# Batches 2 to 7 of a fused attention and bilinear feed-forward kernel: heads grouped by row halves, fewer turning products, and token sums on partitions from batch 2

## The chip, the cores and the metric

The kernel runs on one core of one Trainium2 chip. The metric is the device time of one execution in microseconds (us), as the median of the runs. The engines are TensorE (PE, with its weight loads shown apart as PEld), VectorE (DVE), ScalarE (ACT), GpSimd (POOL) and SyncE (SP).

## The reference

For 8 batches of 8 heads with 576 tokens, head size 64 and 32 memory slots, `phi` gives softmax weights over the slots, and with these every slot gets a mean of the keys and a mean of the values. The queries attend over the 32 slot means. The result, 4608 tokens of 512, goes through a bilinear feed-forward layer with 1536 inner columns.

```python
a = softmax(phi)                               # over the 32 slots, per token
k_m = einsum('bhsm,bhsd->bhmd', a, k)          # means of keys
v_m = einsum('bhsm,bhsd->bhmd', a, v)          # means of values
attn = softmax(q @ k_m.T / sqrt(64))           # (b, h, 576, 32)
x = (attn @ v_m) -> (4608, 512)
out = ((x @ w_a) * (x @ w_b)) @ w_out          # 512 -> 1536 -> 512
```

## The kernel before

The inputs come in by DMA from the POOL queue in a fixed order (`p`, `k`, `v`, `q` of a batch, `w` for columns of w_a and w_b, `o` for w_out). On the chip everything is in 16 bits, and each head's rows lie on 64 partitions: a tile holds two heads per column group, head `2*hp+r` on the partitions from `64*r`, with `r` 0 or 1 and `hp` 0 to 3.

The four stages of a batch are these. **Means:** `kv_sums` (line 277) multiplies the exponentials of `phi` with keys, values and a column of constants, on PE tiles of 64 rows by 32 columns: `tile_position=(64*r, 32*j)` for head slot `j` of group `g`. Two groups of four heads fill two PSUM banks `pkv`. `take_kv` (306) divides by the sums and writes copies into `rep`; `kv_transpose` (321) turns `rep` on PE into `pT`, and DVE copies that to `kvT`, from which each head finds its means on the partitions on which its queries or its weight rows lie. Batches 0 and 1 use other functions for this (`sums`, `transpose`, lines 329 and 353).

**Attention:** `scores` (363) multiplies turned queries with `kvT` on PE tiles of 32 by 32; `exp_scores` writes the exponentials `E`, with slots on partitions and tokens along the row. In batches 0 to 3 the sums over the 32 slots come from PE: `denominators` (391) multiplies `E` with a block matrix of ones into `pD`, ACT takes the logarithm into `L`, and `normalise` (401) has ACT make the reciprocal `R` and DVE (batches 0, 1) or POOL (2, 3) the product `A`. In batches 4 to 7 DVE turns `E` in 32x32 blocks (`e_turn`, 414), so that tokens lie on partitions; `token_sums` (422) reduces and takes reciprocals on DVE, `token_normalise` (429) multiplies, the first part on POOL and the second on DVE, and `a_turn` (435) turns back.

**Up:** `fold` (439) multiplies the value means with rows of w_a and w_b, and `take_fold` (456) moves the product to `vab`; `up_half` (618) multiplies `vab` with `A` into `pa` and `pb`, ACT copies `pa`, and DVE multiplies it with `pb` into the tile `ht`.

**Down:** two chunks of 128 tokens at a time go through w_out with seven products in place of eight (`two_downs`, 542); the sums of blocks that this needs are `w_sums` (`sum_weights`, 512) and `h_sums` (`sum_tokens`, 525).

The order of the work on all engines is written out in the list `PLAN`. In it `2kv` means the means of batch 2, `2km` and `2kvt` the copies and the turning, `2sc` scores, `2e0` exponentials, `2den0` and `2nr0` sums by PE and normalising, `2ed`, `2sm0`, `2tn0`, `2ad` the way by tokens, `2v0` and `2x0a` folding, `a2.3.0` and `b2.3.0` an up product, `dN` N matmuls of the down stage, `h` or `g` a `h_sums` on POOL or DVE, `T` or `V` a `w_sums` on POOL or DVE, `F` and `f` filling matmuls at the start that keep the TensorE clock up. Each engine executes its part of the list in order.

The function that orders the heads decides which rows of the array a head uses:

```python
def head(g, j):
    jj = j ^ g
    return jj % 2, 2 * g + jj // 2     # r, hp
```

So the four heads of a group lie on both row halves by turns.

Of the kernel before, what the change touches and what calls it, by code (L numbers as in the profile page):

```python
# [9 lines left out]
F16 = mybir.dt.float16  # L10
# [3 lines left out]
P = 128  # L14
# [11 lines left out]
f3 F1 O 0exp0 f1 f1 F2 p1 f2 f6 F7 w0:256 f2 f1 k1 f1 F3 0exp1 F5 f2 0qt0 q1.0 0ks0 0ks1 F5 0kt0 0qt1 M F2 0s0  # L26
w256:512 0qt2 0kt1 0e0 0den00 0qt3 0s1 0e1 F4 0den01 1exp0 0vs0 q1.1 0vt0 v1 0vs1 1exp1 F6 0nr00 0den10 0vt1
0den11 0hv0a 0hx0a 0nr10 0hv0b 0hx0b 0nr11 a0.1.0 b0.1.0 a0.0.0 F4 0nr01 1ks0 1ks1 b0.0.0 0hv1a 0hx1a 1kt0 1kt1
1qt0 1qt1 a0.0.1 a0.2.1 F1 b0.0.1 1s0 a0.1.1 0hv1b 1qt2 1qt3 0hx1b 1s1 1e0 1e1 b0.2.1 1den0 a0.2.0 b0.1.1 b0.2.0
1den1 1vs1 1vs0 1vt1 1nr0 1vt0 1nr1 a0.3.1 a0.3.0 1hv1b 1hx1b 1hv0b 1hv0a 1hx0a w512:1024 1hx0b b0.3.1 b0.3.0  # L30
1hv1a 0v1a 1hx1a 0x1a a1.0.0 a1.1.1 a1.1.0 a1.0.1 b1.0.0 b1.1.1 b1.1.0 a1.3.0 b1.0.1 a1.3.1 b1.3.0 b1.3.1 a0.5.0
0v1b 1v1a w1024:1536 0x1b 1x1a a1.2.0 1v1b 0v2a 1x1b o1 0x2a a0.7.1 b0.5.0 b1.2.0 b0.7.1 a0.7.0 b0.7.0 o5 a1.5.0
a1.2.1 b1.2.1 b1.5.0 a0.4.0 a0.6.0 b0.4.0 a0.4.1 a1.4.0 b0.6.0 b1.4.0 a0.9.1 0v2b 1v2b 1v2a 0x2b 1x2b a1.5.1
b0.4.1 1x2a b0.9.1 a0.8.0 a1.4.1 b1.5.1 o2 a0.5.1 a0.6.1 b0.8.0 a0.9.0 b0.6.1 b0.9.0 b1.4.1 a1.7.1 b0.5.1 b1.7.1
a0.8.1 b0.8.1 o0 a1.7.0 a0.10.0 b1.7.0 b0.10.0 a0.11.0 a1.9.0 o3 o4 b0.11.0 g0.0 b1.9.0 a1.6.1 k2 a1.6.0 p2 h0.3
a0.11.1 b1.6.1 b0.11.1 a1.8.1 a0.10.1 b1.6.0 v2 b1.8.1 g0.1 T01 a1.8.0 T00 V20 q2 T21 d1 2exp0 a1.9.1 d3 b0.10.1
p3 a1.10.0 d2 V10 g0.2 V11 d1 b1.9.1 2exp1 d1 a1.11.1 k3 d1 q3 T31 T30 d1 b1.10.0 b1.8.0 d1 b1.11.1 d4 h1.0 d2
2kv d4 2km d3 a1.11.0 d10 a1.10.1 2qt0 3exp0 d1 2kvt d2 h1.1 d1 2qt1 d12 2qt2 d3 2qt3 b1.10.1 g1.2 b1.11.0 v3 d1
2sc 2e0 d1 g1.3 d3 g2.0 d3 2e1 d1 2den0 h2.1 d8 p4 d8 2nr0 2den1 g2.2 2v0 2x0a 2x0b d2 2nr1 d10 2v1 d5 2x1a 3qt0
d3 g2.3 d3 2x1b d1 a2.3.0 a2.2.0 b2.3.0 b2.2.0 q4 k4 v4 a2.5.0 3exp1 b2.5.0 d2 3qt1 d4 a2.0.0 b2.0.0 d3 h3.0  # L40
a2.1.0 a2.4.0 2v2 3kv 3qt3 2x2a 3qt2 b2.1.0 2x2b d2 a2.11.1 a2.6.0 d4 3km a2.8.0 d1 q5 b2.4.0 d3 b2.6.0 d2 4exp0
d5 b2.11.1 d5 h3.1 d2 b2.8.0 a2.11.0 3kvt d2 a2.8.1 a2.7.1 b2.8.1 d2 a2.9.0 b2.7.1 3sc 3e1 3e0 g3.3 d1 b2.11.0
4qt0 a2.7.0 d2 a2.5.1 b2.5.1 b2.7.0 h3.2 3den0 d1 3nr0 4qt3 d1 b2.9.0 d2 a2.0.1 4qt2 a2.10.0 b2.0.1 p5 a2.4.1
b2.10.0 d1 k5 a2.10.1 d3 b2.10.1 d3 h4.0 4exp1 d1 a2.2.1 b2.4.1 3den1 d4 3v1 3x1a 4kv 3v0b 3x1b d3 3x0b d1 3nr1
d6 4km0 h4.1 a2.6.1 b2.2.1 a2.9.1 4qt1 a2.1.1 3v0a 3v2 d1 3x0a d2 3x2a d2 b2.6.1 3x2b d4 a3.9.0 d4 a3.5.0 d2
4km1 h4.2 b2.9.1 d1 a2.3.1 4kvt d1 b2.1.1 d1 b2.3.1 d2 5qt0 4sc a3.11.0 d1 h4.3 b3.5.0 5qt2 d5 4e1 d1 4e0 d1 v5
d6 b3.9.0 a3.0.0 g5.0 d1 h5.1 d3 4ed b3.11.0 d1 a3.3.0 d2 a3.10.1 b3.0.0 h5.2 5exp0 4sm0 q6 a3.1.0 d1 b3.3.0 d4
a3.3.1 d2 p6 d2 b3.10.1 a3.8.1 h5.3 d1 b3.3.1 b3.1.0 a3.6.0 b3.6.0 a3.7.0 a3.10.0 b3.8.1 d1 a3.1.1 b3.7.0 5qt1
d2 a3.8.0 a3.2.0 b3.10.0 d3 5exp1 a3.4.0 d1 b3.8.0 b3.1.1 d2 b3.2.0 k6 b3.4.0 4v0a 5kv 4x0a d1 a3.2.1 5km0
a3.4.1 5km1 d3 h6.0 h6.1 b3.2.1 d1 a3.9.1 d3 a3.5.1 d1 b3.4.1 b3.9.1 d5 4v0b 4x0b 4tn0 4v1 d1 h6.3 d3 4x1a d1  # L50
4x1b d2 a3.11.1 5kvt d1 p7 4sm1 a3.7.1 h6.2 d1 v6 d3 a3.6.1 d2 b3.5.1 b3.11.1 d1 5qt3 4v2 d4 4tn1 a3.0.1 d7 4x2a
4ad 6exp0 d1 b3.0.1 d6 4x2b b3.7.1 a4.11.0 b3.6.1 d1 a4.9.0 6exp1 d1 6qt0 b4.11.0 a4.7.0 a4.4.0 d4 b4.9.0 k7 d1
5sc 5e1 d1 5e0 d1 a4.0.0 d1 b4.4.0 d1 b4.0.0 a4.2.0 b4.2.0 d1 b4.7.0 d3 6qt1 d2 a4.4.1 d2 q7 a4.1.1 b4.4.1 5v0
5x0a 5x0b 6kv 5v1 h7.0 5x1a d3 6km0 a4.10.1 d1 5ed 6km1 d2 h7.3 h7.1 b4.1.1 h7.2 g8.0 d1 5x1b d2 h8.1 d1 a4.6.1
d4 b4.6.1 d4 a4.8.0 a4.5.0 5sm0 d1 v7 d1 h8.2 b4.10.1 a4.8.1 b4.8.0 a4.3.1 b4.5.0 d2 6qt3 d7 5v2 d2 5x2a d2
a4.1.0 d2 b4.3.1 7qt0 a4.3.0 d1 5x2b d1 b4.8.1 d1 7qt2 d1 b4.3.0 a4.5.1 d2 a4.10.0 b4.1.0 d2 6kvt 7exp0 d2 5tn0
d3 5sm1 a4.0.1 b4.5.1 d1 6qt2 d2 b4.0.1 d1 a4.6.0 d3 a4.7.1 d5 h8.3 d1 b4.10.0 d1 7exp1 d2 5tn1 d1 7qt1 a4.11.1
d3 6sc d5 6e1 d5 a4.2.1 d1 b4.7.1 d1 b4.6.0 5ad d1 a4.9.1 d1 h9.0 d1 b4.2.1 d3 6e0 b4.11.1 d1 b4.9.1 d1 a5.2.0
d1 a5.2.1 6ed g9.1 d1 b5.2.0 6v0a 6x0a 6v0b 7kv 6x0b b5.2.1 a5.11.0 b5.11.0 a5.8.0 a5.9.0 b5.8.0 h9.2 d1 7km0 d1
a5.3.0 d1 h9.3 d2 b5.9.0 b5.3.0 d2 a5.6.0 d1 g10.0 d1 h10.1 b5.6.0 a5.3.1 h10.3 d4 b5.3.1 d2 a5.1.0 d5 7qt3 d4  # L60
a5.7.0 d1 7km1 a5.7.1 b5.7.1 d9 b5.7.0 a5.5.0 d3 b5.1.0 d4 6sm0 b5.5.0 d3 a5.0.0 a5.1.1 d1 a5.10.0 d1 b5.0.0
# [12 lines left out]
d1 a7.6.1 d2 b7.11.1 d10 b7.6.1 g16.0 d6 g16.1 d5 g16.2 d1 g17.0 d11 h16.3 d8 h17.1 d24 h17.3 d13 g17.2 d28
# [4 lines left out]
def kernel(  # L79
# [13 lines left out]
    B, H, S, D = q.shape  # L93
    M = phi.shape[3]
# [152 lines left out]
    def head(g, j):  # L247

        jj = j ^ g
        return jj % 2, 2 * g + jj // 2  # L250

    def units(b):

        u = {}
# [51 lines left out]
        def take_kv(gs=range(2)):  # L306

            if gs[0] == 0:
                t["rep"] = mid.tile([P, 6, P], F16, name="rep")
                t["rphi"] = small.tile([P, 2], F32, name="rphi")  # L310
            for g in gs:
                pkv, bank = t["pkv"][g]
                nc.vector.reciprocal(out=t["rphi"][:, g:g + 1], in_=pkv[:, 2 * D:2 * D + 1])
                km = pkv[:, 0:D].rearrange("p (d e) -> p e d", e=2).unsqueeze(2).to_broadcast([P, 2, 4, 32])
                vm = pkv[:, D:2 * D].unsqueeze(1).to_broadcast([P, 2, D])
                for out, x in ((t["rep"][:, 2 * g:2 * g + 2].rearrange("p e (z d) -> p e z d", z=4), km),
                               (t["rep"][:, 4 + g].rearrange("p (z d) -> p z d", z=2), vm)):
                    nc.vector.tensor_scalar(out=out, in0=x, scalar1=t["rphi"][:, g:g + 1], scalar2=None, op0=ALU.mult)
                banks.free(bank)

        def kv_transpose():

            t["kvT"] = mid.tile([P, 6, P], F16, name="kvT")
            pT = banks.tile([P, 6, P], F16, name="pT")
            for x in range(6):
                nc.tensor.transpose(out=pT[:, x, :], in_=t["rep"][:, x], identity=ident)  # L326
            nc.vector.tensor_copy(out=t["kvT"], in_=pT)

        def sums(g, x):

            if g == 0 and x == 0:
                t["kvm"] = mid.tile([P, 2, 2, D], F16, name="kvm")
                t["rphi"] = small.tile([P, 2], F32, name="rphi")
                t["kvT"] = mid.tile([P, 6, P], F16, name="kvT")
# [28 lines left out]
        def scores(gs):  # L363
# [5 lines left out]
            for dh in range(2):  # L369
                for z in range(2):  # L370
                    for g in gs:
                        for j in range(4):
# [4 lines left out]
                                t["kvT"][row:row + 32, 2 * g + dh, M * j:M * j + M],  # L377
# [308 lines left out]
```

## Time and profile before

| | |
|---|---|
| median of 3 runs | 237.14 us (237.03 to 237.19) |
| profiled execution | 237.06 us, span 235.4 us |
| PE busy | 226.6 us, 96% of the span, 3075 matmuls |
| DVE busy | 186.9 us, 79% |
| ACT busy | 152.6 us, 65% |
| POOL busy | 132.0 us, 56% |
| TensorE clock granted | full in nearly all slices |

The span is the time from the first to the last instruction of the program in the profile. The rest of the execution's time, 1.7 us, lies outside of it. Busy PE time is modelled with the matmuls' latency, so that overlapping matmuls count once and short waits can be hidden in it; the distance from one matmul's start to the next tells more.

### The profile page before, as it was taken

The numbers are of one execution on the slowest core, as the hardware profiler recorded it, in microseconds if no ns is written. First come the engines' busy times: TensorE is split into PE (matmuls) and PEld (weight loads), VectorE is DVE, ScalarE is ACT, GpSimd is POOL, SyncE is SP. The second block draws the span as 40 slices with busy tenths as digits, with TensorE's granted clock in tenths as the row PEclk, the third lists the DMA queues.
The fourth block names the chain that finished last, engine by engine and source line by source line (L and its number), as shares of the span: only waits on it lengthen the run. The fifth ranks groups of instructions, "written<-read, shape, count | busy, mean of one in ns | idle before, by whom it ended". The sixth has DMA issues, their size and how long they took to land.

```text
span 235.4 us, 7727 instructions
## 1 busy us (share of the span) xinstructions
PE 226.6 (96%) x3075; PEld 171.4 (73%) x3075; DVE 186.9 (79%) x454; ACT 152.6 (65%) x398; POOL 132.0 (56%) x117
## 2 busy tenths in 40 slices
PE   7988899999999999999999999999999999999993
PEld 4534466788877887888777778788668887888882
DVE  4536699999988889898897998987798687776842
ACT  2265598875697699667787856754884757464330
POOL 6784423895695647776979380665209205535251
PEclk9999999999999999999999999999999999999999
DMA  6999999999999979399699582303030412041264
GB/s 232 235 252 203 207 207 207 205 259 258 214 249 214 198 170 238 66 176 214 117 227 206 133 138 54 92 1 92 1 76 16 92 45 49 1 93 43 57 148 111
DMA packets 25748, 34.12 MB, mean 145 GB/s; under 512 B 2000, under 2 KB 19792, under 8 KB 25712
## 3 DMA queue, kind: packets, MB, share of 16 engines
q0 software_dynamic: 19248, 23.14, 54.0%
q1 hardware_dynamic: 5952, 9.70, 15.6%
q10 hardware_dynamic: 512, 0.79, 1.0%
q8 instruction: 24, 0.39, 0.6%
q14 instruction: 12, 0.10, 0.1%
HBM read 42.47 MB, written 9.44 MB: 221 GB/s over the span
## 4 chain that ended last, share of the span: by engine, by line
PE 86%; DMA 7%; POOL 3%; DVE 1%; issue 0%
PE py L550 21%; PE pb L621 20%; PE pa L621 20%; PE pv L550 10%; PE pva L447 5%; PE px L550 5%; DMA q_sb<-in_q_dram 5%; DMA ht<-in_k_dram 2%; PE pkv L286 2%; PE pscore L375 1%; POOL kv_sb L639 1%; PE pT L326 1%; PE pD L398 1%; POOL wa_sb L159 1%; DVE kv_sb L217 1%; POOL wb_sb L160 1%
## 5 line engine op out<-in xcount | busy, mean ns | idle before, releaser
L625 ACT CAST a_sb<-pa 128x288 f16<-128x288 f32 x192 | 72.3, 407 | 38.1 <-PE pa L621 30.6
L628 DVE TENSOR_TENSOR ht<-a_sb,pb 128x288 f16<-128x288 f16 x192 | 80.1, 447 | 19.6 <-PE pb L621 12.0
L621 PEld LDWEIGHTS <-vab 128*128 128x128 f16 x768 | 73.8, 98 | 19.1 <-issue 3.0
L621 PE MATMUL pb<-A,vab 128*128 128x288 f16 x384 | 71.9, 286 | 0.0
L621 PE MATMUL pa<-A,vab 128*128 128x288 f16 x384 | 71.3, 286 | 0.6 <-DVE A L409 0.4
L534 POOL TENSOR_TENSOR h_sums<-ht 128x768 f16<-128x768 f16 x22 | 36.0, 1640 | 36.5 <-DVE ht L628 36.4
L550 PEld LDWEIGHTS <-h_sums 128*128 128x128 f16 x432 | 41.8, 98 | 9.0 <-issue 1.5
L550 PEld LDWEIGHTS <-ht 128*128 128x128 f16 x324 | 31.0, 98 | 8.5 <-issue 3.5
L460 ACT CAST vab<-pva 128x512 f16<-128x512 f32 (+1 forms) x60 | 31.3, 570 | 7.2 <-PE pva L447 6.8
L550 PE MATMUL py<-w_sums,h_sums 128*128 128x256 f16 x216 | 35.4, 273 | 0.0
L534 POOL TENSOR_TENSOR h_sums<-h_sums,ht 128x768 f16<-128x768 f16 x13 | 21.3, 1639 | 15.1 <-DVE h_sums L534 7.1
L460 DVE CAST vab<-pva 128x512 f16<-128x512 f32 (+1 forms) x44 | 26.8, 635 | 2.9 <-PE pva L447 2.8
L534 POOL TENSOR_TENSOR h_sums<-ht,h_sums 128x768 f16<-128x768 f16 x11 | 18.1, 1643 | 11.0 <-PE pa L621 5.9
L550 PE MATMUL pv<-w_sums,h_sums 128*128 128x256 f16 x108 | 19.3, 273 | 0.0
L557 ACT ACTIVATE u<-py 128x256 f32<-128x256 f32 x36 | 14.0, 390 | 8.1 <-PE py L550 6.2
L550 PE MATMUL px<-wo_sb,ht 128*128 128x256 f16 x108 | 19.0, 273 | 0.0
L550 PE MATMUL py<-wo_sb,ht 128*128 128x256 f16 x108 | 18.9, 273 | 0.0
L550 PE MATMUL py<-w_sums,ht 128*128 128x256 f16 x108 | 18.5, 273 | 0.0
L550 PE MATMUL pv<-wo_sb,h_sums 128*128 128x256 f16 x108 | 18.5, 273 | 0.0
L269 DVE STREAM_TRANSPOSE qT<-q_sb 128x288 f32<-128x288 f32 x32 | 14.5, 465 | 2.1 <-DMA q_sb<-in_q_dram 2.1
L260 ACT ACTIVATE exp_sb<-phi_sb 128x576 f16<-128x576 f32 x16 | 10.8, 687 | 6.0 <-DMA phi_sb<-in_phi_dram 6.0
L211 PE MATMUL pw<-warm 128*128 128x512 f16 (+1 forms) x59 | 13.2, 382 | 1.3 <-DVE warm L180 1.3
(69 smaller groups left out, 247.5 us busy)
## 6 DMA issues: line engine op xcount, KB each, us to landing
out_dram<-o_sb SPq DMA_DIRECT2D x68, 128.0 KB, 2.4
phi_sb<-in_phi_dram POOLq DMA_DIRECT2D x8, 576.0 KB, 7.1
kv_sb<-in_v_dram POOLq DMA_DIRECT2D x8, 576.0 KB, 9.2
kv_sb<-in_k_dram POOLq DMA_DIRECT2D x7, 576.0 KB, 9.9
q_sb<-in_q_dram POOLq DMA_DIRECT2D x6, 576.0 KB, 10.7
wo_sb<-in_moe_w_out_dram POOLq DMA_DIRECT2D x6, 256.0 KB, 15.8
q_sb<-in_q_dram POOLq DMA_DIRECT2D x4, 288.0 KB, 9.7
wa_sb<-in_moe_w_a_dram POOLq DMA_DIRECT2D x2, 512.0 KB, 15.3
```

What stands on the lines that cost most here:

```text
L211: nc.tensor.matmul(pw[:, :cols], warm[:, :P], warm[:, :cols], start=True, stop=True)
L260: nc.scalar.activation(out=t["exp"][:, 2 * z:2 * z + 2, :, :], in_=phis[b][:, 2 * z:2 * z + 2, :].rearrange("p c (i m) -> p c i m", m=M), ...
L269: nc.vector.transpose(out=t["qT"][:, hp, :].bitcast(F32), in_=qs[b][:, hp, :].bitcast(F32))
L286: nc.tensor.matmul(t["pkv"][g][0][32 * j:32 * j + 32, 0:n], t["exp"][64 * r:64 * r + 64, hp, i, :], kvs[b][64 * r:64 * r + 64, 0:3 - given ...
L447: nc.tensor.matmul(t["pva", lo, z][g][0][32 * j:32 * j + 32, 0:hi - lo], t["kvT"][64 * r:64 * r + 64, 4 + g, M * j:M * j + M], w_sbs[z][64 ...
L460: engine_copy(out=vabs[b][z][:, g, lo:hi], in_=pva[:, 0:hi - lo])
L534: engine.tensor_tensor(out=out, in0=in0, in1=in1, op=op)
L550: nc.tensor.matmul(po, lhs[:, i], rhs[:, i], start=first and i == 0, stop=i == KH - 1, skip_group_check=not first)
L557: nc.scalar.mul(out=x, in_=po, mul=scale)
L621: nc.tensor.matmul(ps, vabs[b][x][:, g, P * i:P * (i + 1)], attn[b][:, g, HALF * hf:HALF * (hf + 1)], start=(g == 0), stop=(g == 1))
L625: nc.scalar.copy(out=a_sbs[b, i, hf], in_=ps)
L628: nc.vector.tensor_tensor(out=ht[:, i, t0:t0 + HALF], in0=a_sbs.pop((b, i, hf)), in1=ps, op=ALU.mult)
```

## The change

Heads keep the crossed order in batches 0 and 1. From batch 2 on, group `g` holds the four heads of row half `g`. Each half of `rep` is then filled by one group alone, so that `rep` has 3 columns of 128 in place of 6, three PE products turn it in place of six, and the later stages read `kvT` at other columns. Batches 2 and 3 take the way by tokens (`ed`, `sm`, `tn`, `ad`) in place of `den` and `nr`. For batches 0 and 1 `kvT` lies in a tile of its own. The list `PLAN` is written anew throughout; 46 `h` and 26 `g` become 49 and 23, five `T` and three `V` become six and two.

```diff
-    def head(g, j):
+    def crossed(g, j):
 
         jj = j ^ g
         return jj % 2, 2 * g + jj // 2
 
+    def straight(g, j):
+
+        return g, j
+
     def units(b):
 
+        side = b < 2
+        head = crossed if side else straight
...
-                t["rep"] = mid.tile([P, 6, P], F16, name="rep")
+                t["rep"] = mid.tile([P, 3, P], F16, name="rep")
...
-                km = pkv[:, 0:D].rearrange("p (d e) -> p e d", e=2).unsqueeze(2).to_broadcast([P, 2, 4, 32])
-                vm = pkv[:, D:2 * D].unsqueeze(1).to_broadcast([P, 2, D])
-                for out, x in ((t["rep"][:, 2 * g:2 * g + 2].rearrange("p e (z d) -> p e z d", z=4), km),
-                               (t["rep"][:, 4 + g].rearrange("p (z d) -> p z d", z=2), vm)):
+                km = pkv[:, 0:D].rearrange("p (d e) -> p e d", e=2).unsqueeze(2).to_broadcast([P, 2, 2, 32])
+                half = slice(D * g, D * (g + 1))
+                for out, x in ((t["rep"][:, 0:2, half].rearrange("p e (z d) -> p e z d", z=2), km),
+                               (t["rep"][:, 2, half], pkv[:, D:2 * D])):
...
-            t["kvT"] = mid.tile([P, 6, P], F16, name="kvT")
-            pT = banks.tile([P, 6, P], F16, name="pT")
-            for x in range(6):
+            t["kvT"] = mid.tile([P, 3, P], F16, name="kvT")
+            pT = banks.tile([P, 3, P], F16, name="pT")
+            for x in range(3):
...
-                t["kvT"] = mid.tile([P, 6, P], F16, name="kvT")
+                t["kvT"] = consts.tile([P, 6, P], F16, name=f"kvT{b}")
...
-                                t["kvT"][row:row + 32, 2 * g + dh, M * j:M * j + M],
+                                t["kvT"][row:row + 32, (2 * g if side else 0) + dh, M * j:M * j + M],
...
-                            t["kvT"][64 * r:64 * r + 64, 4 + g, M * j:M * j + M],
+                            t["kvT"][64 * r:64 * r + 64, 4 + g if side else 2, M * j:M * j + M],
```

Of the list, the start and the way of batch 2 from its scores to its first up product, before and after:

```diff
-... 0exp0 f1 f1 F2 p1 ... w0:256 ... k1 ... 0exp1 ... q1.0 0ks0 0ks1 ... M F2 0s0 w256:512 ... 0e0 0den00 ... q1.1 ... v1 ...
+... 0exp0 0qt0 p1 F9 w0:256 ... k1 ... M ... 0exp1 ... 0ks0 0qt2 0ks1 F3 1exp0 0kt0 O 0kt1 ... 0s0 ... w256:512 0e0 0den00 ... q1.0 ... q1.1 F2 v1 ...
...
-2sc 2e0 d1 g1.3 d3 g2.0 d3 2e1 d1 2den0 h2.1 d8 p4 d8 2nr0 2den1 g2.2 2v0 2x0a 2x0b d2 2nr1 d10 2v1 d5 2x1a 3qt0
-d3 g2.3 d3 2x1b d1 a2.3.0
+2sc d2 2e0 d6 2e1 a1.10.1 d1 2v0 g2.0 d2 2ed d2 2x0a h2.1 d4 h2.3 d3 2sm0 d2 h2.2 d2 2tn0 d4 2x0b 3exp0 d5 2v1 d3
+2x1a 2sm1 q4 d1 3qt0 d1 2tn1 d9 b1.10.1 d5 2ad d12 2x1b d11 a2.2.0
```

## The prediction

> **What bounds the kernel now.** I read the page's shares first, then the busy time by windows, then the waits, and last the timeline of PE for the pace of single matmuls.
>
> ```profile
> PE 226.6 (96%) x3075; PEld 171.4 (73%) x3075; DVE 186.9 (79%) x454; ACT 152.6 (65%) x398; POOL 132.0 (56%) x117
> ```
>
> ```profile
> 40.00:60.00 20.00, 20.00 (x253) 15.78 (x252) 19.27 (x50) 14.43 (x40) 15.29 (x13) 1.00 1.19 236
> 60.00:80.00 20.00, 20.00 (x305) 15.69 (x303) 17.80 (x44) 15.26 (x40) 15.34 (x14) 1.00 1.11 223
> 80.00:100.00 20.00, 20.00 (x333) 15.47 (x331) 17.48 (x43) 16.91 (x45) 11.62 (x10) 1.00 0.77 162
> 100.00:120.00 20.00, 20.00 (x274) 15.64 (x272) 17.73 (x44) 13.70 (x36) 16.48 (x14) 1.00 0.84 167
> ```
>
> The columns of a window are its length, then PE, PEld, DVE, ACT and POOL busy, the granted clock, the DMA share and GB/s. From 40 us on PE has no gap. The waits agree: those that end before a PE instruction sum to 4.4 us in the whole span and none of them lies after 40 us. The longest:
>
> ```profile
> PE pva L447 <- DMA wa_sb<-in_moe_w_a_dram: 1.3, 1, 1.3
> ```
>
> Modelled ends could hide small holes, so I looked at starts. The chain of waits shows four `pa` matmuls in 0.49 us, 0.122 us apart, all the way through, and six `py` in 0.66, 0.109 apart. So from 40 us to the last matmul at 231 us the kernel is a row of PE work without holes, and each matmul less there is time less, if the others keep up. Before about 30 us the weights and batch 1's inputs arrive at their own pace, and PE waits and runs filling matmuls. DVE is the next engine: 96% busy from 40 to 60 us without making PE wait, 89% from 60 to 120.
>
> **What goes from PE.** The paces come from the timeline:
>
> ```profile
> 59.56 0.50 PE L326 MATMUL pT<-ident,rep 128*128 128x128 f16 x6
> 65.83 0.41 PE L398 MATMUL pD<-E,ones 128*128 128x288 f16 x2
> 15.77 0.10 PEld L358 LDWEIGHTS <-kvm 128*32 128x32 f16 x4 [0.53 <-DVE kvm L350]
> 15.77 0.24 PE L358 MATMUL pT<-ident,kvm 128*32 128x128 f16 x4 [0.42 <-DVE kvm L350]
> ```
>
> One turning product alone takes 0.219 us, six take 0.50, so each further one costs (0.50-0.22)/5 = 0.056. Three fewer in six batches: 18 x 0.056 = 1.01 us. One `pD` takes 0.286, two 0.41, so 0.123 each; batches 2 and 3 had four each: 8 x 0.123 = 0.98 us. All of it lies after 40 us. Together 1.99 us. The instruction lists of the two kernels bear this out: 3075 matmuls become 3049, and every other kind keeps its count, the 59 filling ones too.
>
> **What the new head order does on PE.** The sums, scores and folds have the same matmuls on the same set of tiles, but neighbours in `kv_sums` and `scores` are now four tiles on the same rows. The trace has that case already: the four `pT` of line 358 use all 128 rows and four column groups; their weight loads, 95 ns each, take 0.10 us together, and the matmuls 0.24 against 0.226 for one. So same-row neighbours overlap, and I take 0. From below: 288 columns take 0.122 us, so a batch's nine rounds of 192 columns take at least 0.73 of the 0.77 us that the chain shows for its sums; at most 0.2 us are to be won in six batches. From above I take the doubled block, 6 x 0.77 + 6 x 0.40 for the scores = 7.0 us, which the row for line 358 makes very unlikely.
>
> The Trainium skill (TensorE: Matmul & The Clock Gate, Part 3, "The mechanism") says that a weight load overlaps a running matmul only where the row group differs. That would speak against this change: three of four neighbours in the sums would wait for each other, as an estimate 54 x 0.08 us in each of six batches, some 26 us, and the sum would be about 261 us. The four loads in 0.10 us contradict it for different column groups, and the measurement decides.
>
> **What DVE gets.** Its rows:
>
> ```profile
> L318 DVE TENSOR_SCALAR rep<-pkv,rphi 128x256 f16<-128x256 f32 x12 | 5.8, 484 | 0.4
> L318 DVE TENSOR_SCALAR rep<-pkv,rphi 128x128 f16<-128x128 f32 x12 | 4.1, 342 | 0.0
> L327 DVE COPY kvT<-pT 128x768 f16<-128x768 f16 x6 | 3.3, 555 | 0.7 <-PE pT L326 0.7
> L426 DVE TENSOR_REDUCE sum<-E 128x20 f32<-128x640 f16 x4 | 3.2, 809 | 0.0
> L437 DVE STREAM_TRANSPOSE A<-E 128x576 f32<-128x576 f32 x4 | 3.1, 769 | 0.0
> L416 DVE STREAM_TRANSPOSE E<-E 128x576 f32<-128x576 f32 x4 | 3.1, 768 | 0.0
> L433 DVE TENSOR_TENSOR E<-E,sum 128x512 f16<-128x512 f16 x4 | 2.7, 677 | 0.0
> L426 DVE TENSOR_REDUCE sum<-E 128x16 f32<-128x512 f16 x4 | 2.7, 675 | 0.0
> ```
>
> A batch by tokens costs DVE 0.77 + 0.81 + 0.675 + 0.677 + 0.77 and two reciprocals of 0.28 and 0.25 = 4.2 us. Batches 2 and 3: +8.4. A batch with half the copies saves twice 0.484 - 0.342 and twice 0.342 - 0.284 (a 128x64 scaling on line 350) = 0.4, and the 128x384 copy lies between 0.287 (128x256) and 0.555, say 0.35, so 0.2 more: -0.6 in each of six batches. One `V` goes to POOL, and the new list has six `g` of 0.55 where the old had ten up to 120 us (three fewer in all). From 40 to 120 us DVE had 72.3 us; now 72.3 + 8.4 - 4 x 0.6 - 4 x 0.55 - 0.55 = 75.6 in 78 us, 97%. That is what DVE did from 40 to 60 us, but for four times as long. This is the step I trust least. I charge 0.3 us for it: near nothing, by the row of 40 to 60 us with 96% and no PE wait; the other end is under the rivals.
>
> **ACT and POOL.** ACT loses eight logarithms of 0.427 and four `R` of 0.70: -6.2 us, all beside PE. POOL loses four products of 1.28, gains two of 1.27, three `h` of 1.64 and one `T` of 1.65: +4.0 us on an engine that is 56% busy, nothing while two places hold. First, `T30 h1.0 T31` now end late: o3 lands at 47.7, then `T10`, two loads, `T30`, `h1.0`, `T31` end near 60.0, and PE reaches their product at about 60.2; if this slips, PE waits by as much. Second, `2tn0` stands behind `h2.1 h2.3 h2.2`, 4.9 us. From batch 2's scores to its first up product lie 75 down matmuls (8.2 us), four folds of 0.28 and two up halves, together 9.8 us of PE work. The way by tokens, 1.42 + 0.77 + 1.09 + 1.27 + 0.77 = 5.3 us, and what is left of those `h` fit with about 1 us to spare. `2ad` waits on DVE for `2tn0`, with the evacuations of the down stage behind it. Batch 3 has 13 us for the same way.
>
> **The start.** DMA stays the clock here. `1exp0` now stands before `0e0` on ACT, and phi of batch 1 lands at 16.2 (its wait on the timeline), so batch 0's attention comes later: from 16.2 on ACT has 0.63 + 0.71 + 0.43 + 0.71 + 0.43 + 0.45 and more in a row, 8.6 us with its waits for `pD`, and the first up product starts near 24 in place of 19.2. Before, PE then waited 1.3 us for w_a columns that end at 24.3; these now stand ahead of a q half and land about 1.4 us earlier. Counted from the lists with the paces above, PE has 13.0 us of work ahead of the first fold of columns 512 on, before 13.6, and those columns land at 32.4; before, PE came there at about 33.2. So the start can bring at most 0.8 us, and I see no more loss than 0.7 from the later attention, as ACT is full till 33. I take 0.
>
> **The sum.** 237.06 (span 235.4 and 1.7 around it; the median is 237.14) - 1.99 + 0.3 = 235.4 us.
>
> **The rivals.** (1) DVE becomes the bound from 50 to 120 us. In the windows from 60 to 120 it was idle 7 us, 6 of them waits for PE, ACT and their like. PE never waited then, so most of that was slack. If a DVE that works in order can't shed more than half of its 7.7 idle us of 40 to 120, it needs 75.6 + 3.9 = 79.5 us where PE needs 78, and the gain is down to 0.5; the change turns slower when more than 4.4 us stay. With all 7.7 it is 83.3, so 5.3 - 2.0 = 3.3 slower, 240.4; in the middle 238.5. For it: two saturated engines in a row. Against: 40 to 60 us, where 0.7 us idle was enough. Chance 0.16. (2) The gain is eaten by the start or by a tight place in the new list (`T31`, `2tn0`): 237.1, within 0.2% of now, 0.08. (3) Same-row neighbours do cost: 244, 0.03. (4) The change doesn't do what it says: excluded by the instruction lists.
>
> **How the numbers follow.** Forecast 0.73, rivals 0.16, 0.08, 0.03. 0.2% (0.5 us) is about what a measurement tells from no change. The forecast's own range is 234.6 (start 0.5 better, no charge for DVE) to 236.5 (1.1 lost on DVE). To hold eight in ten it must reach into rival 1: up to 238.3. The forecast's 0.73 is 0.72 faster and 0.01 the same; rival 1 gives 0.13 slower, 0.02 faster and 0.01 the same; rival 2 half the same and half slower; rival 3 slower. In all 0.74 faster, 0.06 the same, 0.20 slower.
>
> **What would show it.** Right: 8 `pD` and 18 `pT` fewer, a batch's sums still 0.77 us and its scores 0.40, the last matmul 1.5 to 2 us earlier, DVE at 95 to 98% from 40 to 120 with no PE wait over 0.3 us. Wrong: PE waits for `ht`, `vab` or `A` from DVE, or for `w_sums`, between 50 and 120; sums that take 1 us and more; a PE that reaches batch 2's sums later than 56.3 us.

## The result, and the profile after

The changed kernel takes 237.71 us (median of 20 runs, 237.43 to 237.93) where the kernel before, run beside it, takes 237.15. The ratio is 1.0019, 95% interval 1.0011 to 1.0027: 0.2% slower: little, but clear of no change. The forecast was 235.4. The profiled execution has a span of 235.8 us, before 235.4.

The page's shares say that the work changed nearly as forecast:

```profile
PE 225.0 (95%) x3049; PEld 169.2 (72%) x3049; DVE 191.4 (81%) x464; ACT 147.2 (62%) x386; POOL 136.7 (58%) x119
```

26 matmuls fewer, ACT 5.4 us less, DVE 4.5 and POOL 4.7 us more. The windows show where the time went instead. Columns: length, then PE, PEld, DVE, ACT, POOL busy, granted clock, DMA share, GB/s.

```profile
40.00:60.00 20.00, 20.00 (x251) 15.85 (x250) 19.06 (x51) 13.80 (x38) 17.60 (x15) 1.00 1.21 222
60.00:80.00 20.00, 20.00 (x302) 15.44 (x300) 19.67 (x47) 13.45 (x35) 19.03 (x16) 1.00 1.09 244
80.00:100.00 20.00, 20.00 (x300) 15.71 (x299) 18.79 (x47) 14.99 (x39) 11.68 (x11) 1.00 1.10 228
100.00:120.00 20.00, 18.26 (x274) 14.15 (x272) 17.99 (x42) 13.31 (x35) 15.10 (x10) 1.00 0.49 109
```

DVE is busy 75.5 us from 40 to 120; the forecast said 75.6. Yet PE has no hole in the two windows where DVE is fullest (95% and 98%). Its only hole in these windows, 1.74 us, is in the last one, where DVE is at 90%. The waits name it:

```profile
PE pT L332 <- DVE ht L634: 1.7, 1, 1.7
```

Batch 5's three `pT` products need a PSUM bank that VectorE's `ht` product frees. They start at 118.98, when the `ht` product of 118.49 has ended. The timeline of VectorE (start, us, engine, line, operation, out<-in) shows what ran just ahead of that one:

```profile
115.93 2.64 DVE L439 TENSOR_TENSOR E<-E,sum 128x512 f16<-128x512 f16 x1
118.49 0.44 DVE L634 TENSOR_TENSOR ht<-a_sb,pb 128x288 f16<-128x288 f16 x1
```

The by-token product of batch 4 (`4tn1`) takes 2.64 us. The row of line 439 shows how odd that is (duration ns min/median/max):

```profile
L439 DVE TENSOR_TENSOR E<-E,sum x6: 682/684/2640, 69.2 to 187.4; 128x512 f16<-128x512 f16 x6
```

And this is GpSimd at that time:

```profile
115.54 0.81 POOL L138 DMA_DIRECT2D phi_sb<-in_phi_dram  x1
116.36 1.65 POOL L540 TENSOR_TENSOR h_sums<-ht 128x768 f16<-128x768 f16 x1
```

The product ends at 118.57, 0.56 us after the sum `h6.3` (116.36 to 118.01). Other rows have the same mark: a VectorE instruction with both inputs in SBUF beside a GpSimd sum, ending about half a microsecond after it. The trace of before has one, which I had passed over. On VectorE and on GpSimd:

```profile
226.29 1.17 DVE L534 TENSOR_TENSOR h_sums<-ht,h_sums 128x768 f16<-128x768 f16 x1
```

```profile
225.40 1.64 POOL L534 TENSOR_TENSOR h_sums<-ht 128x768 f16<-128x768 f16 x1
```

1.17 in place of 0.55. In the kernel before, the product `4tn1` started at 119.13 and GpSimd's sum ended at 119.10: they missed each other by 0.03 us.

```profile
119.13 0.65 DVE L433 TENSOR_TENSOR E<-E,sum 128x512 f16<-128x512 f16 x1
```

```profile
117.44 1.66 POOL L534 TENSOR_TENSOR h_sums<-ht,h_sums 128x768 f16<-128x768 f16 x1
```

The new start has a hold of another kind. VectorE's two casts of batch 0's keys (one input in SBUF) took 1.43 us together in the kernel before, from 5.77 us, beside an idle GpSimd. In the changed kernel GpSimd issues four DMAs from 5.00 to 8.25 and then clears a tile, and the two take 3.07:

```profile
5.74 3.07 DVE L217 CAST kv_sb<-ht 128x1152 f16<-128x1152 f32 x2 [2.13 <-DMA ht<-in_k_dram]
```

All ten traces with the new start have 2.97 to 3.17, the casts starting from 5.64 to 5.83 and always done between 8.80 and 8.82; all six with the old start have 1.43. No run separates what this costs PE.

For an account of the rest I take the start of each up product and subtract the PE work that the list puts ahead of it, at the forecast's paces. What is left is the time lost so far; the paces are a little long, so that it can fall along the way, and only the difference of two kernels counts. Before it is 19.43 us at 50 us and 18.45 at the end. After it is 19.79 at 50 us, 20.00 at 72, 19.57 at 109, 21.50 at 122 and 21.11 at the end. So the change lost 2.66 us more: 0.36 at the start, 0.16 by 72 us, 1.9 at 119, and 0.2 in pieces, among them a wait of 0.31 us for batch 7's `A` at 189.6. With 1.99 us less work at these paces that makes +0.67; the last matmul starts at 231.64 in place of 230.98.

### The profile page after: what moved, and what is told of

Same layout as the page of the kernel before. It is cut to its first block, busy times and chain, and to the rows that moved or that the text cites. A ratio compares the mean times of both kernels' runs of the same rounds, so it can differ in the third digit from the quotient of the medians.

```text
span 235.8 us, 7665 instructions
## 1 busy us (share of the span) xinstructions
PE 225.0 (95%) x3049; PEld 169.2 (72%) x3049; DVE 191.4 (81%) x464; ACT 147.2 (62%) x386; POOL 136.7 (58%) x119
## 4 chain that ended last, share of the span: by engine, by line
PE 84%; DMA 8%; DVE 3%; POOL 1%; issue 1%; ACT 0%; POOLq 0%
PE py L556 20%; PE pa L627 20%; PE pb L627 19%; PE pv L556 10%; DMA q_sb<-in_q_dram 8%; PE pva L453 5%; PE px L556 5%; PE pkv L292 2%; PE pscore L381 1%; DVE E L439 1%; DVE ht L634 1%; DVE qT L275 1%; PE pT L332 0%; POOL phi_sb L138 0%; PE pk L346 0%
## 5 line engine op out<-in xcount | busy, mean ns | idle before, releaser
L634 DVE TENSOR_TENSOR ht<-a_sb,pb 128x288 f16<-128x288 f16 x192 | 78.7, 444 | 15.9 <-PE pb L627 8.7
L627 PE MATMUL pb<-A,vab 128*128 128x288 f16 x384 | 69.9, 286 | 0.3 <-DVE kvT L367 0.3
L540 POOL TENSOR_TENSOR h_sums<-ht 128x768 f16<-128x768 f16 x27 | 44.1, 1642 | 30.3 <-DVE ht L634 29.7
L556 PEld LDWEIGHTS <-h_sums 128*128 128x128 f16 x432 | 41.3, 98 | 10.3 <-issue 3.2
L556 PE MATMUL py<-w_sums,h_sums 128*128 128x256 f16 x216 | 34.6, 273 | 0.0
L540 POOL TENSOR_TENSOR h_sums<-h_sums,ht 128x768 f16<-128x768 f16 x12 | 19.7, 1643 | 13.6 <-PE pa L627 12.6
L540 POOL TENSOR_TENSOR h_sums<-ht,h_sums 128x768 f16<-128x768 f16 x10 | 16.4, 1640 | 8.5 <-PE py L556 5.9
L556 PE MATMUL px<-wo_sb,ht 128*128 128x256 f16 x108 | 18.2, 273 | 0.0
L556 PE MATMUL pv<-w_sums,h_sums 128*128 128x256 f16 x108 | 18.1, 273 | 0.0
L556 PE MATMUL py<-w_sums,ht 128*128 128x256 f16 x108 | 17.3, 273 | 0.0
```

What stands on the lines that cost most here:

```text
L540: engine.tensor_tensor(out=out, in0=in0, in1=in1, op=op)
L556: nc.tensor.matmul(po, lhs[:, i], rhs[:, i], start=first and i == 0, stop=i == KH - 1, skip_group_check=not first)
L627: nc.tensor.matmul(ps, vabs[b][x][:, g, P * i:P * (i + 1)], attn[b][:, g, HALF * hf:HALF * (hf + 1)], start=(g == 0), stop=(g == 1))
L634: nc.vector.tensor_tensor(out=ht[:, i, t0:t0 + HALF], in0=a_sbs.pop((b, i, hf)), in1=ps, op=ALU.mult)
```

## The experiments

My theory after this reading: the change's parts are worth what was forecast, and a block of VectorE by one GpSimd sum takes it back. The rival: VectorE has too much to do (the forecast's rival 1), and the long product is a symptom.

**The sum moved off GpSimd.**

```diff
-b3.5.1 d7 a4.0.0 4v2 d1 h6.3 4x2a 4x2b h7.0 d5 5sc
+b3.5.1 d7 a4.0.0 4v2 d1 g6.3 4x2a 4x2b h7.0 d5 5sc
```

> The changed kernel with one token of the list altered: the sum h6.3 is made by VectorE (g6.3) and no longer by GpSimd. Theory (blocking): in the changed kernel the E<-E,sum product of batch 4 on VectorE (115.93 us) took 2.64 us in place of 0.68 because GpSimd's h6.3 ran from 116.36 to 118.01; without it the product takes 0.68, the wait of 1.74 us ahead of batch 5's three pT transposes is gone, and the time falls by 1.6 to 1.9 us from 237.7, to about 235.9. Rival (VectorE has too much to do there): VectorE gets 0.55 us more work ahead of the same ht product, the product still takes over 2 us or the wait stays near 1.7, and the time stays at 237.7 or rises to 238.2.

235.89 us, ratio to before 0.9944 (0.9931 to 0.9958). VectorE has more to do and the hole is gone:

```profile
115.87 0.68 DVE L436 TENSOR_TENSOR E<-E,sum 128x512 f16<-128x512 f16 x1
```

```profile
100.00:120.00 20.00, 20.00 (x291) 15.76 (x289) 18.01 (x47) 14.78 (x39) 13.46 (x9) 1.00 0.48 108
```

One token of the list is worth 1.8 us. The rival is out: with 0.55 us more on VectorE there is no wait.

**The sum 0.95 us earlier.**

```diff
-5kvt p7 d1 5qt3 ... 4v2 d1 h6.3 4x2a
+5kvt h6.3 p7 d1 5qt3 ... 4v2 d1 4x2a
```

> The changed kernel with h6.3 moved ahead of the issue of p7 on GpSimd: the sum then starts near 115.5 and ends near 117.2 in place of 118.0, and the DMA issue follows it. Theory (blocking by the sum): the E<-E,sum product still starts near 115.9 and ends 0.55 us after the sum, near 117.75, so takes about 1.8 us in place of 2.64; PE's wait falls from 1.74 to about 0.9, and the time from 237.7 to about 236.9. Rival (blocking by the issue of the DMA too): the product stays blocked until the issue of p7 ends near 118.0, takes over 2.4 us, and the time stays within 0.2 of 237.7.

236.86 us, 0.9985 (0.9976 to 0.9993). The product ends 0.55 us after the sum again, and a DMA issue that follows does not hold it:

```profile
115.78 1.82 DVE L436 TENSOR_TENSOR E<-E,sum 128x512 f16<-128x512 f16 x1
```

```profile
115.41 1.64 POOL L537 TENSOR_TENSOR h_sums<-ht 128x768 f16<-128x768 f16 x1
117.00 0.81 POOL L135 DMA_DIRECT2D phi_sb<-in_phi_dram  x1
```

PE's wait is 0.93 us. So the price follows the length of the block, 0.85 us less for 0.82 us.

**GpSimd as busy, but writing only.**

```diff
-4v2 d1 h6.3 4x2a
+4v2 d1 m6.3 4x2a
...
+        elif x == "m6.3":
+            for _ in range(2):
+                nc.gpsimd.memset(h_sums[12][:, 3], 0.0)
```

> The changed kernel with h6.3 replaced by two memsets of the same tile on GpSimd: an instruction pair of about the same length (0.8 us each) that writes SBUF and reads nothing. It leaves out the sum h6.3 (zeros stand in its place). Theory (GpSimd's reads block VectorE's two-input product): the product takes 0.68 us though GpSimd is as busy beside it, PE's wait is gone, time about 235.9. Rival (any access by GpSimd blocks): the product takes over 2 us again and the time stays at about 237.7.

235.79 us, 0.9940 (0.9927 to 0.9952). The product takes 0.68 us from 115.82 on, with a memset beside it from 116.23. What blocks this product is not that GpSimd works, but that it reads.

**The same block put into the kernel before.**

```diff
-5kvt d1 p7 4sm1 a3.7.1 h6.2 d1 v6 d3 a3.6.1
+5kvt d1 p7 4sm1 a3.7.1 d1 v6 k7 h6.2 d3 a3.6.1
```

(`k7` leaves its old place.)

> The kernel before, with the same blocking made on purpose: GpSimd's order p7, h6.2, v6, k7 becomes p7, v6, k7, h6.2, so that the sum h6.2, which ended at 119.10 and 0.03 us before VectorE's E<-E,sum product of batch 4 (119.13 to 119.78), runs from about 118.9 to 120.6. Theory: the product ends 0.55 us after the sum, near 121.15, so takes about 2.0 us in place of 0.65; VectorE's queue is 1.35 us late there, PE waits for an ht product behind it, and the time rises by 0.3 to 1.3 us over 237.15. Rival (blocking is not what stretched the product, or VectorE has room for it): the product takes 0.65 to 0.7 us, or PE shows no new wait over 0.3 us, and the time stays within 0.2 of 237.15.

238.28 us, 1.0048 (1.0035 to 1.0060): the old kernel loses 1.1 us by the order of GpSimd's queue alone.

```profile
119.40 2.01 DVE L431 TENSOR_TENSOR E<-E,sum 128x512 f16<-128x512 f16 x1
```

```profile
119.20 1.65 POOL L532 TENSOR_TENSOR h_sums<-ht,h_sums 128x768 f16<-128x768 f16 x1
```

PE waits 0.96 us at 122.8 for batch 4's `A`, which stands behind the product. With this the theory predicted four runs in size and sign.

**The first part alone.** The changed kernel's code with the list of before.

```diff
+        head = crossed if side else straight
...
 PLAN as before: 2den0 2nr0 2den1 2nr1 ... 3den0 3nr0 3den1 3nr1
```

> The first part of the change alone: from batch 2 on the heads go straight and three products turn the means, on the list of before (batches 2 and 3 still sum their weights by halves, with pD products). 18 fewer pT at 0.056 is 1.0 us less TensorE work. Theory (straight order costs nothing, what the change lost was lost in the new list): 237.15 - 1.0 = 236.1, unless this list, moved by under 1 us, meets a block of VectorE by GpSimd of its own; the E<-E,sum product near 118 is the one to look at. Rival (straight order costs TensorE time somewhere that the paces did not show): 237 or more with no product of VectorE over 0.8 us.

236.07 us, 0.9959 (0.9946 to 0.9971): 1.06 us less than the 237.13 beside it, for 18 `pT` at 0.056 = 1.01. The last matmul starts 1.02 us earlier. No two-input product of VectorE is longer than before.

**The new list with the old heads.** The code of before with the new list.

```diff
-        head = crossed if side else straight
+        head = crossed
...
-            for x in range(3):
+            for x in range(6):
```

> The new list, with batches 2 and 3 summed by tokens, but heads crossed and six products to turn the means as before. Theory: 18 pT more at 0.056 and VectorE's wider copies, so 1.0 us over the changed kernel's 237.7: 238.7, with the same block of the E<-E,sum product of batch 4 (over 2 us) if GpSimd and VectorE meet as they do there; without the block 237.0. Rival (the crossed order itself is the cheaper): 237.5 or less with the block still there.

239.74 us, 1.0108 (1.0093 to 1.0124). That is 2.03 more than the changed kernel, twice what I expected. The 18 `pT` are 1.0 of it. PE also waits three times for a bank that a copy into `rep` frees (0.18, 0.28, 0.32 us) and for `qT` once (0.21), since VectorE's wider copies come late in a list made for narrow ones. The block is there (2.31 us for the product) and 0.33 us cheaper, which two later waits of 0.2 us for `ht` make up.

**The second part undone**, on the version with `g6.3`.

```diff
-2ed ... 2sm0 ... 2tn0 ... 2sm1 ... 2tn1 ... 2ad
+2den0 ... 2nr0 ... 2den1 ... 2nr1
```

(Batch 3 likewise.)

> The new list with the sum h6.3 on VectorE (235.9 us), and batches 2 and 3 back to sums by halves: pD products, logarithm and exponent on ScalarE, product on GpSimd; the turns of E and A and the sums by tokens are left out. Theory (TensorE sets the time and the second part of the change is worth its eight pD): 0.98 us more, 236.9. Rival (the by-token sums cost VectorE time that PE pays for, so undoing them gains): 235.9 or less. A third reading, that GpSimd with 2.6 us more work per two batches blocks VectorE or comes late with A: over 237.3.

239.39 us, 1.0094 (1.0080 to 1.0108): 3.5 us over the version with `g6.3`. The eight `pD` are 0.98 of it. The third reading holds for the rest. GpSimd, with the products back on it, is late with sums:

```profile
PE pv L553 <- POOL h_sums L537: 0.6, 1, 0.6
PE py L553 <- POOL h_sums L537: 0.6, 1, 0.6
```

From start to start of the matmuls these two cost 0.80 us each, and a wait for `u` at 70 us another 0.43. Some 0.5 us of the 3.5 are left without a cause.

**The second part by hand in the old list.**

```diff
-2den0 h2.1 d8 p4 d8 2nr0 2den1 g2.2 2v0 ... 2nr1 ... g2.3 d3 2x1b
+2ed h2.1 d8 2sm0 p4 d8 2tn0 2sm1 h2.2 2v0 ... 2tn1 ... h2.3 2ad d3 2x1b
```

(Batch 3 likewise: `3ed`, `3sm0`, `3sm1 3tn0`, `3tn1`, `3ad`.)

> The list of before with straight heads and three products (236.07 us), and batches 2 and 3 summed by tokens, put into that list by hand: 2den0 becomes 2ed, 2nr0 becomes 2sm0 and 2tn0, 2den1 becomes 2sm1, 2nr1 becomes 2tn1, 2ad and h2.3 (on GpSimd in place of VectorE, as h2.2) where g2.3 stood; batch 3 likewise with 3ad where 3nr1 stood. Theory (eight pD less is 0.98 us wherever VectorE has room): 235.1. Rival (without a list made for it the 3.2 us more per batch on VectorE make PE wait for A, rep or ht between 60 and 90): 236.5 to 239.

241.17 us, 1.0172 (1.0159 to 1.0184): slower than I had allowed for. PE waits for `o_sb`, `A` and `ht` at 67, 72 and 90 us, 1.4 to 2.0 us each from start to start. The windows say what kind of shortage it is:

```profile
60.00:80.00 20.00, 17.64 (x278) 13.37 (x277) 17.99 (x44) 12.27 (x30) 15.70 (x14) 1.00 1.04 210
80.00:100.00 20.00, 17.75 (x274) 12.98 (x272) 18.03 (x45) 12.83 (x34) 12.81 (x10) 1.00 0.82 172
```

VectorE is busy 90% while PE waits, and 98% in the changed kernel's second window where PE does not. So here the order decides, not the sum of VectorE's work. What eight `pD` less are worth by themselves can't be had from these runs, as neither list suits both ways; only their work is known.

**The old start.** The version with `g6.3`, its first entries replaced by the first 180 of the list of before; the others follow in the new order.

```diff
-F6 f5 0exp0 0qt0 p1 F9 w0:256 ...
+f3 F1 O 0exp0 f1 f1 F2 p1 f2 f6 F7 w0:256 ... a0.8.1 b0.8.1
```

> The new list with h6.3 on VectorE (235.9 us) and the start taken from the list of before: its first 180 entries, up to b0.8.1, and then the entries of the new list that are left, in their order. Theory (the new start loses about 0.36 us, by the position of TensorE in the list at 50 us): 235.5, first up product near 19.2 us in place of 23.3. Rival (the start is level, the difference was made good later): 235.8 to 236.0; or, with the work shifted by some tenths, a new meeting of GpSimd and VectorE, seen as a two-input product over 0.8 us, and over 236.

237.86 us, 1.0030 (1.0019 to 1.0041). The first `pkv` comes at 55.6 us in place of 56.0, so the old start is the faster one by 0.4. Then a new block takes it back, and more:

```profile
54.76 2.64 DVE L520 TENSOR_TENSOR w_sums<-wo_sb,w_sums 128x768 f16<-128x768 f16 x1
```

```profile
54.55 0.75 POOL L135 DMA_DIRECT2D phi_sb<-in_phi_dram  x1 [0.35 <-ACT a_sb L628]
55.31 1.66 POOL L520 TENSOR_TENSOR w_sums<-wo_sb,w_sums 128x768 f16<-128x768 f16 x1
```

PE waits 0.47 for `w_sums` and 1.22 for `rep` behind it.

**Batch 7's turn earlier.**

```diff
-7tn1 b6.5.0 b6.1.0 a6.8.1 h12.3 7ad a6.5.1
+7tn1 b6.5.0 7ad b6.1.0 a6.8.1 h12.3 a6.5.1
```

> The new list with h6.3 on VectorE (235.89 us) and batch 7's turn of A (7ad) issued one b half and one a half earlier on VectorE, right behind 7tn1 and b6.5.0. In the changed kernel TensorE loses 0.31 us at 189.6 waiting for it. Theory: that wait goes and nothing else moves, 235.6. Rival (the wait only turns into one for the b6.1.0 product, which now stands behind the turn's 0.77 us): 235.8 to 236.0.

235.84 us, 0.9949 (0.9937 to 0.9961). The rival holds: at the same place PE now loses 0.28 us to an `ht` product. This and the version with `g6.3` (235.89) can't be told apart; they are the fastest here and beat both kernels.

**A shorter piece of the old start**, 90 entries, on the version with the earlier turn.

```diff
-F6 f5 0exp0 0qt0 p1 F9 w0:256 ...
+f3 F1 O 0exp0 f1 f1 F2 p1 f2 f6 F7 w0:256 ... b0.1.1 b0.2.0
```

> The kernel of the run before, with the start taken from the list of before for its first 90 entries only (up to b0.2.0 of the two first batches, near 24 us) and the new list's order from there on. The longer piece gained 0.4 us up to the first pkv (55.6 in place of 56.0) and lost 1.7 in waits for VectorE between 55 and 61. Theory (the new start is the slower one and the loss came from the seam's place near 50 us): first pkv near 55.6 and 0.3 to 0.4 us less than the run before, 235.2 to 235.3. Rival (any gain at the start is given back before 61 us since VectorE is the late one there): 235.5 to 235.8 with a wait of PE for rep or w_sums; or, where the shift sets up a new block of a two-input product, over 236.

238.46 us is the median of twelve runs, which lie in three groups: three at 236.0 to 236.2, seven at 238.4 to 238.6, two at 239.6 and 240.0. The ratio, 1.0025 (0.9998 to 1.0053), leaves the last two out and is not clear of no change. The profile is of the longest run, at 240.0:

```profile
50.57 3.44 DVE L538 TENSOR_TENSOR h_sums<-ht 128x768 f16<-128x768 f16 x1
```

```profile
50.40 0.78 POOL L140 DMA_DIRECT2D kv_sb<-in_k_dram  x1
51.17 0.75 POOL L148 DMA_DIRECT2D q_sb<-in_q_dram  x1
51.94 1.65 POOL L521 TENSOR_TENSOR w_sums<-wo_sb,w_sums 128x768 f16<-128x768 f16 x1
```

Whether the other groups had this block was not seen, as none of their runs was profiled; the group at 236.0 would still not gain the 0.4 us. So the old start's 0.4 us did not reach the end in either attempt.

**When does the hold begin?** Here, in the run with 180 old entries and in the changed kernel, the product makes no progress while GpSimd still issues a DMA, before the sum begins. An issue alone does not hold it (with `g6.3` the product ran beside the same issue in 0.68 us). The test:

```diff
-4x1a 5kvt p7 d1 5qt3
+4x1a 5kvt p7 k7 d1 5qt3
```

(`k7` leaves its later place; `h6.3` is still next behind it on GpSimd.)

> The changed kernel with the issue of k7 moved up, right behind that of p7 and ahead of the sum h6.3: GpSimd then issues two DMAs from 115.5 to 117.1 and sums from 117.1 to 118.75, while VectorE's E<-E,sum product of batch 4 starts near 115.9. Theory A (a sum that stands ready behind a DMA issue holds VectorE from some 0.15 us after that issue began until the sum ends): the product takes 3.4 us (ends 0.56 after the sum), PE's wait ahead of the pT transposes grows from 1.74 to about 2.5, time 238.4. Theory B (the sum holds VectorE from its own start only): the product is done at 116.6 before the sum begins, takes 0.68, the wait is gone, 235.9 to 236.1.

```profile
115.83 3.39 DVE L436 TENSOR_TENSOR E<-E,sum 128x512 f16<-128x512 f16 x1
```

```profile
115.45 0.81 POOL L135 DMA_DIRECT2D phi_sb<-in_phi_dram  x1
116.25 0.75 POOL L139 DMA_DIRECT2D kv_sb<-in_k_dram  x1
117.02 1.65 POOL L537 TENSOR_TENSOR h_sums<-ht 128x768 f16<-128x768 f16 x1
```

3.39 us: theory A. The product, begun 1.19 us before the sum and behind two issues, ends 0.55 us after it. The time is 239.96 us, 1.0107 (1.0088 to 1.0126), 1.6 us over theory A's. The granted clock accounts for that: it fell after a PE wait of 2.49 us.

```profile
121.00:122.00 1.00, 1.00 (x6) 0.60 (x5) 0.73 (x3) 0.87 (x3) 0.00 (x0) 0.50 1.10 220
122.00:123.00 1.00, 1.00 (x6) 0.67 (x5) 1.00 (x3) 0.28 (x1) 0.00 (x0) 0.50 1.14 253
```

With 0.77 in the microsecond before and 0.52 in the one after, these lose 0.23 + 0.50 + 0.50 + 0.48 = 1.7 us, about the rest of the time. (One of the six runs took 238.61, at a mean clock of 0.996 where the others had 0.989 to 0.993, so the loss does not come every time.) The changed kernel's wait of 1.74 us left the clock at 1.00.

**The collision by itself.** Two probes behind the end of the version with `g6.3`, on free tiles. Each trial is one VectorE instruction, released by ScalarE, and a GpSimd one released before or after it.

```diff
+        for d in ("tt", "tt", "copy", "ts", "turn", "sum"):
+            for p, order in (("", "d"), ("tt", "dwp"), ("tt", "pd"), ("set", "pd")):
+                for x in "dpww" + order:
+                    go(x)
+                dve[d]()
+                if p:
+                    pool[p]()
```

(`go` is a ScalarE copy into the operand that `d`, VectorE, or `p`, GpSimd, waits for; `w` a delay. The second probe has `dp` for `dwp` and, for the memset, `dp` for `pd`.)

> The kernel with h6.3 on VectorE, and behind its end six groups of four trials on free tiles: one VectorE instruction on 128x1536 fp16 (sum of two tiles, twice; copy; product with a scalar; turn of 32x32 blocks; sum over 32) alone, with GpSimd's sum of two 128x768 tiles started some 0.5 us after it, with that sum started just ahead of it, and with a GpSimd memset started just ahead of it. The span grows by the trials; only their durations are read. Theory (what blocks is a read of SBUF by GpSimd against a VectorE instruction that needs both inputs from SBUF): the sum of two tiles is blocked by GpSimd's sum in either order, for as long as that runs (1.64 us), and not by the memset; the other four are untouched by all. Rival one (who starts first holds): the sum of two tiles is blocked only where GpSimd started ahead, and GpSimd's sum waits where VectorE did. Rival two (the copy and the product with a scalar, where VectorE runs faster than one element a cycle, use the same path): these two are blocked too.

> The same trials behind the end as in the probe before, with GpSimd's sum, and in the fourth trial its memset, started 0.2 to 0.4 us behind VectorE's instruction in place of 1.0 us. What the first probe showed: started together with GpSimd's sum, VectorE's sum of two tiles, its copy and its product with a scalar all waited for its end, the turn and the sum over 32 did not, and the memset held back the copy and the product with a scalar alone. If who starts first holds: in the second trial VectorE's sum of two tiles, copy and product take what they take alone (0.96, 0.56, 0.62 us) and GpSimd's sum takes 0.3 to 0.8 us more than its 1.63. If GpSimd always wins: VectorE's take over 2 us and GpSimd's 1.63.

In the first probe the later start came 1.0 us behind, when the shorter instructions were done, so the second probe repeated it at 0.2 us. "First" is released first; the two then start within 0.04 us. Durations in us, GpSimd's own in brackets where it grew (its sum takes 1.63, its memset 0.74 alone):

| VectorE, 128x1536 fp16 | alone | GpSimd sum first | sum just behind | memset first | memset just behind |
|---|---|---|---|---|---|
| sum of two tiles | 0.96 | 2.44 | 0.96 (2.27) | 0.96 | 0.96 |
| copy | 0.56 | 2.04 | 0.56 (1.82) | 1.12 | 0.56 (1.03) |
| product with a scalar | 0.62 | 2.04 | 0.62 (1.88) | 1.11 | 0.62 (1.09) |
| turn of 32x32 blocks | 0.98 | 0.98 | 0.98 | 0.98 | 0.98 |
| sum over 32 | 1.75 | 1.75 | 1.75 | 1.75 | 1.75 |

My theory fell in two places: the copy and the product with a scalar are blocked as well, and by the memset too; and the sum of two tiles is not blocked in either order. Who gets hold first keeps it to nearly its end, and the other one waits; it is no sharing.

## Why the prediction was wrong

**PE's work: right for the `pT`, not tested for the `pD`.** The list of before with the first part gained 1.06 us for 1.01 forecast. The eight `pD` are gone by the count, but no run shows their 0.98 us alone: the account of lost time uses the forecast's own paces and can't test them.

**Straight heads: right, at 0.** A batch's sums, and its scores, in the changed kernel on PE:

```profile
74.55 0.95 PE L292 MATMUL pkv<-kv_sb,exp_sb 64*32 64x192 f16 x72
80.50 0.47 PE L381 MATMUL pscore<-qT,kvT 32*32 32x288 f16 x32
```

The same rows of the kernel before say 0.95 (at 73.99) and 0.47 (at 62.55). The 32 score products on four row groups and four column groups start some 3 ns apart within each half: same-row neighbours still overlap. The 26 us that the prediction worked out from the Trainium skill's sentence (TensorE: Matmul & The Clock Gate, Part 3, "The mechanism") did not come; for tiles in different column groups these rows speak against it.

**VectorE's work: 75.5 us for 75.6, but partly by luck, and the rival built on it was the wrong one.** VectorE at 98% did not stop PE. The step counts one duration for each kind of instruction, and 0.3 us for it all. In the changed kernel four products with two inputs in SBUF are longer than their kind, by 3.2 us together (0.46 at 61.58, 0.45 at 69.16, 1.96 at 115.93, 0.32 at 170.94), and the casts of the start by 1.6; before, one product was, by 0.6. So 2.9 of the 75.5 us are time held, not work. Of the four products only that at 115.93 made PE wait. The sign "PE waits for `ht`" came true, but its cause was this hold and not rival 1's full VectorE: 0.55 us more work on VectorE, with the hold gone, made the wait go.

**GpSimd's work, "+4.0 us on an engine that is 56% busy, nothing while two places hold": this is the step that failed.** Both places held, `T31` and `2tn0` made nobody wait. But the forecast put at nothing what GpSimd's sums do to VectorE: one of them stretched `4tn1` from 0.68 to 2.64 us, PE waited 1.74 us behind it, and moving that sum brought back 1.8 us (237.71 to 235.89). GpSimd's time is not free to VectorE where VectorE has two inputs in SBUF. The rows for it were there: 1.17 us beside a 0.55 row, and the 0.03 us between sum and product at 119.1. The price of a bad meeting is the rest of the sum, up to 1.64 us, or 2.0 with one DMA issue ahead (2.64 less 0.68) and 2.7 with two (3.39 less 0.68); the new list has some 23 `g`, two `V` and six `tn1` on VectorE that can meet 49 `h`, six `T` and six `tn0`. A rival "one `tn1` meets an `h`", about 1.9 less some slack, ends at 237.3 or a little under and would have stood near the measured time.

The Trainium skill has the rule (SBUF — State Buffer, "Who interferes with whom"): a VectorE instruction with two SBUF inputs contends with a GpSimd instruction that reads SBUF, not with one that only writes it; a copy or a product with a scalar in its two-port modes contends with GpSimd as such; and whichever issues first holds the shared ports for the whole instruction. The probes agree with it: 2.44 in place of 0.96 for the sum of two tiles beside GpSimd's sum, 0.96 beside the memset; 1.12 in place of 0.56 for the copy beside the memset; GpSimd's sum at 2.27 in place of 1.63 the other way round. In the traces the hold can begin before the start that they show for GpSimd's sum, as with the 3.39 us above.

**The start: 0 forecast, 0.36 us lost.** Within its bounds. The first up product came at 23.27 (about 24 forecast). The wait for the w_a columns fell from 1.32 to 0.38 us, while in the chain of waits PE stands 0.37 us for `kvm` at 31.2 and 0.42 for `vab` at 32.7. That these make up the 0.36 is argued, not shown, and so is any part of the held casts.

**The sum.** Forecast -1.7, measured +0.56. Of the 2.3 us between, 1.8 is the block (by `g6.3`), 0.36 the start, and 0.36 in pieces, less the 0.3 charged: 2.2. Rival 2, "a tight place in the new list", comes nearest in time (237.1), by the wrong places. That 237.71 lies under the 238.3 allowed for rival 1 is luck as well: VectorE's amount of work was not what cost the time.

## What to carry to other kernels

Where VectorE and GpSimd work at the same time, look down each VectorE row for its longest instruction (min/median/max), and at what GpSimd did beside it; a maximum far over the median, ending a fixed time after a GpSimd instruction, points to a block (a row of two instructions, as that of the casts, has no median to trust: compare it with another run's). When work is moved to an idle GpSimd, or an instruction list is ordered anew, count the pairs that can meet, and keep a reading GpSimd instruction, and a DMA issue with one behind it, away from the VectorE products that the critical engine waits for. A fix can be one token: look for it before giving up the change.

## What I had not expected of the hardware

A GpSimd sum that stands ready behind a DMA issue holds VectorE before it starts. Over all traces here, products with two inputs in SBUF that started 0.05 to 0.14 us after the issue began were free (0.68 us at 90.26 in the changed kernel, issue at 90.13); those at 0.17 to 0.73 us after it were held to the sum's end, five of five; with no ready sum behind, none was. So less than a tenth of a microsecond decides on 2 us. It may be what splits the run groups of the short old start; that is not shown. A cast is another case: in the new start two were held beside DMA issues that no sum followed (3.07 us in place of 1.43).

PE waits of 2.49 us (two issues) and 2.14 us (the profiled run of the short old start) were each followed by some 3 us at a granted clock of 0.50, 1.7 us of work lost. The wait of 1.74 us cost nothing beyond itself.
